# A planned instruction order for capped attention and a gated MLP: the planner's costs, landings and due times replaced

## The chip, the core and the metric

The kernel runs on one core of a Trainium2 chip. The core has five engines with a queue of instructions each: TensorE (PE, matrix products), VectorE (DVE, element-wise work), ScalarE (ACT, functions of one operand), GpSimd (POOL, hardly used here) and SyncE (SP, which issues nearly all transfers). An engine takes its instructions in the order in which they stand; one that waits holds up all behind it. The metric is the device time of one execution in microseconds (us), and lower is better.

## The reference, cut to what matters

```python
# 4 batches, 12 heads, 448 tokens, head size 64
scores = q @ k.T / sqrt(64)
scores = cap * tanh(scores / cap)
attn = exp(scores - max) ; attn = attn / (sum(attn) + 1e-9)
x = (attn @ v), heads side by side            # 1792 tokens x 768
g = x @ w_gate ; val = x @ w_val              # 768 x 1536 each
out = (g * sigmoid(g) * val) @ w_out          # 1536 x 768
```

The weights come as 64-bit floats and are narrowed to 32 bits on the chip. The large products run with operands that are split into two 16-bit halves, a high one and a low one.

## The kernel before

**Stages.** The attention comes first. A unit is one pair of heads of one batch; two units make a quad, and there are 12 quads. A quad has seven score tiles of 128 x 896: three of each unit and one (`MID`) with the rest of both. For each tile TensorE multiplies queries and keys (`qk`), ScalarE takes the tangent out of PSUM into a slot of SBUF (`tanh`) and the exponential in place (`exp`). Then TensorE multiplies with the values (`av` three times for each unit, `avt` for the rest) and with ones for the sums of the rows (`sum`), for which VectorE first adds three tiles (`sa`). The sums go over three transfers: `cp` copies them out of PSUM, `rl` spreads them over the partitions, `rec` takes the reciprocal on VectorE, `rs` writes it to memory, and `rld` reads it back for each unit, so that `x` can multiply the product that `xk` had copied out. The score tiles have two PSUM buffers (`sc`): the scores of a tile can be written when the tangent of the tile two before has read its own.

Behind the attention come 13 steps of gate and value products (`step`) and two passes of output products (`outs`). They use a scheme with seven products for a 2 x 2 block product; the blocks of x are differences of each other (`T1` to `T4`). For each product VectorE and ScalarE make a high half (`XH`, `wH`) and a low half (`XL`, `wL`) of the operands, and combine the partial results (`c1`, `c11`, `cu` and so on). The first step uses the first half of the batches only; in the second step the products of the second half begin. The weights are narrowed beside all this (`narrow`, `quarter`).

**The order.** `Plan.run` makes it when the kernel is built. Every operation has a cost on each engine that can run it, the operations that it depends on, the buffers that it takes, and a due time. The planner simulates the engines: of the operations that could start within 0.05 us of the earliest one, it takes the one with the earliest due time. The instructions are then written out in that order, and each engine keeps it, whatever the times turn out to be on the chip. TensorE's order in the attention stage isn't left to the planner: the list `line` at the end of the kernel ties each operation to the one before. Between the pieces of a quad there stand those of the quad before, in this order: one `qk`, three `av`, two `qk`, three `av`, one `qk`, `sum`, two `qk`, `avt`, one `qk`.

**Names that the change touches.** `QUAD` is the step of the quads in the due times, `tile_at` the due time of a tile in it (a seventh of `QUAD` each). `SWITCH` is a cost when TensorE goes from one kind of matmul to another, `LAG` and `LAT` are delays between the end of an operation and the start of one that depends on it, `FAR` is added to the landing of some transfers (`rl`, `rs`, `rld` are those of the reciprocals, `ld` are loads of weights), and `ISSUE` is the time in which SP issues one. `TAGS` gives each score tile the SBUF slot for its tangent. The due times of a tile at time z are z + 1.0 for `tanh` and z + 2.8 for `exp`.

Of the kernel before, what the change touches and what calls it, by code (L numbers as in the profile page):

```python
# [42 lines left out]
QUAD = 13.5  # L43
# [14 lines left out]
SWITCH = 0.17  # L58
# [21 lines left out]
class Plan:  # L80
# [3 lines left out]
    LAG = {  # L84
        ("PE", "PE"): 0.0, ("ACT", "ACT"): 0.13, ("DVE", "DVE"): 0.13, ("POOL", "POOL"): 0.13, ("ACT", "DVE"): 0.16,
        ("DVE", "POOL"): 0.16, ("ACT", "POOL"): 0.18, ("POOL", "ACT"): 0.07, ("POOL", "DVE"): 0.08, ("ACT", "PE"): 0.25,
    }

    FAR = {"rl": 1.4, "rs": 1.4, "rld": 1.4}
    ISSUE = {"rld": 0.96}  # L90
# [13 lines left out]
    def run(self):  # L104
# [69 lines left out]
        while ready:  # L174
            t0, cands = 1e18, []
            for k in ready:
# [5 lines left out]
                for t, d, e, x in o["opts"]:  # L182
                    s = max(t, r, free[e])
                    if e == "PE" and kind(k) != last:
                        s += SWITCH
# [36 lines left out]
def tile_capped_attention_gated_mlp(ctx: ExitStack, tc: tile.TileContext, qd, kd, vd, cap, eye, w1, w2, out):  # L222
# [104 lines left out]
    mm_us = 6 * 188 / 1000.0  # L327
# [95 lines left out]
    def blocks(w):  # L423
        g0, g1 = 2 * w * NCC, (2 * w + 1) * NCC
        for c in range(HALF):
# [14 lines left out]
            for p, (_, _, _, z) in PROD.items():  # L440
# [12 lines left out]
                if z in PLAIN:  # L453
                    n = 3 * PLAIN.index(z) + c
                    square(("qx", z, w, c), 2, win_at[3] + 10.0 * n + 5.0 * w, 0.58, lambda z=z, c=c: T["xs", z, w, c][:, 0], [("p", 3 + n // 2, 1, 4)], ("XH", z, w, c))

    def step(s):
# [46 lines left out]
        for half in range(2):  # L504
            if 1 in ws:
                square(key("q", half), 0, at[0] - 6.0 + 2.0 * half, 0.85, lambda half=half: gate(half).rearrange("p a b -> p (a b)"), full[half], ("XH", "B11", s // NFC, 0))
# [9 lines left out]
        for w in ws:  # L516
# [40 lines left out]
            for b in range(2):  # L557
# [22 lines left out]
                square(("qh", g, f), 3, max(end, z + 2.0) + 1.0, 0.58, lambda b=b, w=w: T["cc", s, w, b], [key("va", w, b)], ("XH", "B11", 0, 0) if s < NFC - 1 else ("oH", 0, 1, 0))  # L580
# [26 lines left out]
    def outs(pr):  # L607
# [54 lines left out]
        for n, (p, d) in enumerate(OUT_ORDER):  # L662
# [13 lines left out]
            if pr:  # L676
                square(("qo", p, d), 1, tp - 6.5, 0.85, lambda p=p, d=d: T["wf", "o", 1, p, d].rearrange("p a b -> p (a b)"), [("ld", "o", 1, p, d)], ("oH", 1, p, 0))
# [86 lines left out]
    TAGS, idle = {}, [f"w{n}" for n in range(6)] + ["B60", "B61", "B62", "B70", "B71"]  # L764
    for q in range(len(QUADS)):
        if q == len(QUADS) - 1:
            idle = [x for x in idle if x[0] == "B"] + ["B22", "B32", "B52"]
        old = TAGS.get(q - 1, [])
        TAGS[q] = [None] * NT
        for i in sorted(range(NT), key=lambda i: spot(q, i)):  # L770
            TAGS[q][i] = idle.pop(0)
# [477 lines left out]
```

## Time and profile before

| what | us |
|---|---|
| median of 3 runs | 603.34 |
| lowest and highest run | 602.14 and 603.51 |
| the profiled execution | 604.18 |
| span from its first to its last instruction | 602.3 |
| TensorE busy | 591.7 |
| VectorE busy | 505.9 |
| ScalarE busy | 418.4 |

The profiled execution's time has 1.9 us around its span. Times in the rows are counted from the start of the span. TensorE's matmuls are pipelined and their ends are modelled, so where consecutive matmuls start says more than how long they were busy. TensorE's granted clock is 0.999 of its full 2.4 GHz. PE is TensorE, DVE VectorE, ACT ScalarE, SPq SyncE's queue.

### The profile page before, as it was taken

What the parts mean: (1) busy time and instruction counts of PE and PEld (TensorE: products, weight loads), DVE (VectorE), ACT (ScalarE), POOL (GpSimd) and SP (SyncE); (2) the same over time, 40 slices, a digit from 0 to 9 for tenths busy, and PEclk for the clock granted to TensorE, in tenths of its full rate; (3) what the DMA queues carried; (4) which work ended last, traced back from release to release, by engine and by line L of the source; (5) the groups of instructions that cost most, each with busy time, mean ns of one, the idle gap of its engine ahead of it and who ended that gap; (6) DMA issues with size and microseconds to landing.
All of it is one profiled execution on the core that took longest, in us unless ns stands there. A gap on an engine that the chain in (4) does not pass through costs nothing.

```text
span 602.3 us, 9584 instructions
## 1 busy us (share of the span) xinstructions
PE 591.7 (98%) x3333; PEld 279.8 (46%) x3333; DVE 505.9 (84%) x869; ACT 418.4 (69%) x725; POOL 1.6 (0%) x11
## 2 busy tenths in 40 slices
PE   7999999999999999999999999999999999999997
PEld 2333333333345555555555555555455555555553
DVE  2678899899898998888989888989979999898840
ACT  6999989899858855756648476656757766685611
POOL 1000000000000000000000000000000000000000
PEclk9999999999999999999999999999999999999999
DMA  8676676755423365877786766586968598546121
GB/s 252 207 237 192 186 223 212 217 153 149 126 86 101 125 173 153 265 203 229 198 239 215 217 211 190 171 274 206 347 235 319 170 331 287 192 135 234 35 78 66
DMA packets 69598, 118.08 MB, mean 196 GB/s; under 512 B 13604, under 2 KB 47524, under 8 KB 69541
## 3 DMA queue, kind: packets, MB, share of 16 engines
q1 hardware_dynamic: 69362, 117.32, 61.4%
q8 instruction: 28, 0.46, 0.3%
q14 instruction: 30, 0.24, 0.1%
q10 hardware_dynamic: 146, 0.07, 0.0%
q0 software_dynamic: 32, 0.00, 0.0%
HBM read 81.79 MB, written 35.48 MB: 195 GB/s over the span
## 4 chain that ended last, share of the span: by engine, by line
PE 84%; DMA 6%; DVE 5%; ACT 2%; SPq 2%; issue 1%; ACTq 0%; DVEq 0%
PE b L528 10%; PE b L530 10%; PE b L529 10%; PE sc L886 7%; PE b L704 7%; PE b L703 7%; PE b L705 7%; PE av L831 6%; PE om L528 4%; PE om L530 4%; PE om L529 4%; DMA w<-w 3%; DMA r<-c 2%; PE b L918 2%; PE av L912 1%; PE om L704 1%
## 5 line engine op out<-in xcount | busy, mean ns | idle before, releaser
L528 PE MATMUL b<-A,w 128*128 128x448 f16 x252 | 88.8, 352 | 0.4 <-ACT c L255 0.4
L529 PE MATMUL b<-A,w 128*128 128x448 f16 x252 | 88.8, 352 | 0.0
L530 PE MATMUL b<-A,w 128*128 128x448 f16 x252 | 88.8, 352 | 0.0
L528 PEld LDWEIGHTS <-w 128*128 128x128 f16 x504 | 49.3, 98 | 46.8 <-issue 0.7
L529 PEld LDWEIGHTS <-w 128*128 128x128 f16 x504 | 49.3, 98 | 46.4 <-issue 0.7
L530 PEld LDWEIGHTS <-w 128*128 128x128 f16 x504 | 49.3, 98 | 46.0
L255 ACT ACTIVATE c<-b 128x448 f32<-128x448 f32 x54 | 29.0, 538 | 44.4 <-PE b L705 22.9
L528 PE MATMUL om<-B,w 128*128 128x448 f16 x144 | 50.8, 352 | 0.0
L529 PE MATMUL om<-B,w 128*128 128x448 f16 x144 | 50.8, 352 | 0.0
L530 PE MATMUL om<-B,w 128*128 128x448 f16 x144 | 50.8, 352 | 0.0
L886 PE MATMUL sc<-c,c 64*128 64x448 f32 (+1 forms) x192 | 45.2, 577 | 2.4 <-ACT w L890 1.5
L546 DVE TENSOR_TENSOR c<-c,b 128x448 f32<-128x448 f32 x60 | 37.1, 619 | 8.6 <-PE b L530 3.2
L262 DVE TENSOR_TENSOR A<-A,A 128x448 f16<-128x448 f32 (+3 forms) x55 | 43.7, 823 | 0.1
L255 ACT ACTIVATE w<-B 128x768 f16<-128x768 f32 x32 | 26.9, 840 | 22.9 <-PE b L705 17.9
L890 ACT ACTIVATE w<-sc 128x896 f32<-128x896 f32 x42 | 36.9, 917 | 7.2 <-PE sc L886 7.0
L890 ACT ACTIVATE B<-sc 128x896 f32<-128x896 f32 x42 | 36.9, 921 | 5.0 <-PE sc L886 4.9
L262 DVE TENSOR_TENSOR w<-B,w 128x768 f16<-128x768 f32 x39 | 37.0, 953 | 2.2 <-ACT w L255 2.2
L893 ACT ACTIVATE B<-B 128x896 f32<-128x896 f32 x42 | 38.4, 959 | 0.1
L893 ACT ACTIVATE w<-w 128x896 f32<-128x896 f32 x42 | 38.2, 955 | 0.1
L704 PE MATMUL b<-A,w 128*128 128x448 f16 x108 | 38.1, 352 | 0.0
L528 PE MATMUL b<-B,w 128*128 128x448 f16 x108 | 38.1, 352 | 0.0
L530 PE MATMUL b<-B,w 128*128 128x448 f16 x108 | 38.1, 352 | 0.0
(138 smaller groups left out, 1233.3 us busy)
## 6 DMA issues: line engine op xcount, KB each, us to landing
w<-w SPq DMA_DIRECT2D x72, 384.0 KB, 3.7
hidden<-c SPq DMA_DIRECT2D x48, 224.0 KB, 3.1
B<-w_S SPq DMA_DIRECT2D x24, 384.0 KB, 4.3
w<-wf SPq DMA_DIRECT2D x16, 384.0 KB, 4.9
B<-w SPq DMA_DIRECT2D x15, 384.0 KB, 3.4
th<-parts SPq DMA_DIRECT2D x48, 112.0 KB, 2.9
A<-hidden SPq DMA_DIRECT2D x12, 448.0 KB, 5.7
B<-hidden SPq DMA_DIRECT2D x12, 448.0 KB, 3.8
```

Source lines behind the costliest of these rows:

```text
L255: nc.scalar.activation(out_, in_, AF.Copy, scale=1.0 if scale is None else scale)
L262: ENG[e].tensor_tensor(out_, a, b, op=ALU.subtract)
L528: nc.tensor.matmul(o, lhsT=wh, rhs=xh, start=first, stop=False, skip_group_check=True)
L529: nc.tensor.matmul(o, lhsT=wl, rhs=xh, start=False, stop=False, skip_group_check=True)
L530: nc.tensor.matmul(o, lhsT=wh, rhs=xl, start=False, stop=end, skip_group_check=True)
L546: nc.vector.tensor_tensor(z, z, T["ps", s, w, b][:, :S], op=ALU.add)
L703: nc.tensor.matmul(o, lhsT=wh, rhs=xh, start=first, stop=False, skip_group_check=True)
L704: nc.tensor.matmul(o, lhsT=wl, rhs=xh, start=False, stop=False, skip_group_check=True)
L705: nc.tensor.matmul(o, lhsT=wh, rhs=xl, start=False, stop=end, skip_group_check=True)
L886: nc.tensor.matmul(z[rows, h, :S], lhsT=T["rk", w][r, keys], rhs=T["rq", w][r], start=True, stop=True)
L890: nc.scalar.activation(T["t", q, i], T["sc", q, i][:, :, :S], AF.Tanh, scale=icapr)
L893: nc.scalar.activation(T["t", q, i], T["t", q, i], AF.Exp, scale=capr)
```

## The change

The diff replaces constants of the planner and two rules in it.

- The step of the quads goes from 13.5 to 13.1; the due time of an exponential from z + 2.8 to z + 5.0.
- The switch cost of TensorE depends on the kind of matmul that it leaves.
- Delays between dependent operations on ScalarE and VectorE are 0.04, and after an operation the engine is free 0.1 (ScalarE) or 0.085 (VectorE) before its end. Before, it was free at the end, and a dependent one came 0.13 to 0.16 later.
- The transfers of the reciprocals land 2.0 later than their data would by the planner's rate, not 1.4; loads of weights 1.5 later, not 0. Issuing takes other times, 2.45 for the four transfers of a quad's values, not 0.48.
- The slots for the tangents come from a ring of eleven in order of the tiles, with seven fixed ones for the last quad. Before, slots were handed on from a list of idle ones.
- Some costs: squares 0.08 more, `tanh` 0.917 and `exp` 0.953, `sum` 1.27, and 189 ns for a matmul of the products.

The operations, their dependences, their tiles and TensorE's order in the attention stage stay.

```diff
-QUAD = 13.5
+QUAD = 13.1
...
-SWITCH = 0.17
+SWITCH = {"sc": 0.206, "av": 0.15, "sh": 0.16, "sum": 0.0, "mm": 0.16}
...
-    LAG = {
-        ("PE", "PE"): 0.0, ("ACT", "ACT"): 0.13, ("DVE", "DVE"): 0.13, ("POOL", "POOL"): 0.13, ("ACT", "DVE"): 0.16,
-        ("DVE", "POOL"): 0.16, ("ACT", "POOL"): 0.18, ("POOL", "ACT"): 0.07, ("POOL", "DVE"): 0.08, ("ACT", "PE"): 0.25,
-    }
-
-    FAR = {"rl": 1.4, "rs": 1.4, "rld": 1.4}
-    ISSUE = {"rld": 0.96}
+    LAG = {("PE", "PE"): 0.0, ("ACT", "PE"): 0.08, ("DVE", "PE"): 0.08}
+    LAG |= {(a, b): 0.04 for a in ("ACT", "DVE") for b in ("ACT", "DVE")}
+    OVERLAP = {"ACT": 0.1, "DVE": 0.085}
+
+    FAR = {"rl": 2.0, "rs": 2.0, "rld": 2.0, "ld": 1.5}
+    ISSUE = {"rld": 1.26, "loadv": 2.45, "rl": 0.65, "rs": 0.4, "ld": 0.45, "st": 0.54}
...
-                        s += SWITCH
+                        s += SWITCH[last]
...
-                free[e] = s + self.ISSUE.get(k[0], 0.48)
+                free[e] = s + self.ISSUE.get(k[0], 0.48) * (2 if k[0] == "loadq" and d > 1.0 else 1)
...
-                free[e] = s + d
+                free[e] = s + d - self.OVERLAP.get(e, 0.0)
...
-    mm_us = 6 * 188 / 1000.0
+    mm_us = 6 * 189 / 1000.0
...
-    TAGS, idle = {}, [f"w{n}" for n in range(6)] + ["B60", "B61", "B62", "B70", "B71"]
...
+    RING = [*(f"w{n}" for n in range(6)), "B60", "B61", "B62", "B70", "B71"]
...
-            tag = TAGS[q][i]
+            tag = (["B22", "B32", "B52", "B60", "B61", "B62", "B70"][spot(q, i)] if q == len(QUADS) - 1 else RING[(NT * q + spot(q, i)) % len(RING)])
...
-            op(("tanh", q, i), z + 1.0, {"ACT": 0.92}, tanh, [("qk", q, i)], [(tag, users)])
-            op(("exp", q, i), z + 2.8, {"ACT": 0.95}, expo, [("tanh", q, i)])
+            op(("tanh", q, i), z + 1.0, {"ACT": 0.917}, tanh, [("qk", q, i)], [(tag, users)])
+            op(("exp", q, i), z + 5.0, {"ACT": 0.953}, expo, [("tanh", q, i)])
...
-        op(("sum", q), av_at(q, 2), {"PE": 1.15}, sums, [("sa", u, 1), ("sa", v, 1), ("exp", q, MID)], [("b2", [("cp", q)])])
+        op(("sum", q), av_at(q, 2), {"PE": 1.27}, sums, [("sa", u, 1), ("sa", v, 1), ("exp", q, MID)], [("b2", [("cp", q)])])
```

## Rows read from the trace of the kernel before

**Rows 1.** The page, busy times: engine, us, share of the span, instructions.

```profile
PE 591.7 (98%) x3333; PEld 279.8 (46%) x3333; DVE 505.9 (84%) x869; ACT 418.4 (69%) x725; POOL 1.6 (0%) x11
```

**Rows 2.** The chain that ended last: start, duration, what (us).

```profile
27.34 1.70 PE sc L886 x12
...
40.40 1.70 PE sc L886 x12
...
62.63 1.27 PE b L918 x24
...
67.41 6.07 DMA r<-c
...
89.35 1.27 PE b L918 x24
...
102.41 1.27 PE b L918 x24
...
107.24 4.91 DMA r<-c
...
128.90 1.27 PE b L918 x24
...
137.39 5.18 DMA parts<-r
```

**Rows 3.** Windows: stretch, length, busy us (instructions) of each engine, clock, DMA.

```profile
core 0: us, PE busy (x) PEld busy (x) DVE busy (x) ACT busy (x) POOL busy (x), PEclk, DMA share, GB/s
...
154.00:168.00 14.00, 12.65 (x110) 4.60 (x108) 14.00 (x24) 13.31 (x19) 0.00 (x0) 1.00 0.34 103
...
196.00:203.00 7.00, 7.00 (x39) 3.62 (x38) 7.00 (x15) 5.37 (x12) 0.00 (x0) 1.00 0.10 35
...
392.00:424.00 32.00, 31.59 (x168) 16.24 (x166) 27.93 (x55) 17.08 (x40) 0.00 (x0) 1.00 0.80 244
```

**Rows 4.** TensorE's timeline: start, us, line, operation, tiles, [idle before <-releaser].

```profile
4.22 3.91 PE L886 MATMUL sc<-c,c 64*128 64x448 f32 x12
...
10.66 1.92 PE L886 MATMUL sc<-A 64*128 64x448 f32 x8 [1.46 <-ACT w L890]
...
14.96 1.02 PE L886 MATMUL sc<-c,c 64*128 64x448 f32 x4
...
159.69 0.59 PE L886 MATMUL sc<-c,c 64*64 64x448 f32 x2 [0.78 <-ACT B L890]
...
161.24 4.73 PE L831 MATMUL av<-B,B 128*64 128x448 f32 x24 [0.57 <-DVE B L257]
```

**Rows 5.** ScalarE's timeline (L890 tangent, L893 exponential, L255 cast), in five places.

```profile
8.02 1.78 ACT L893 ACTIVATE w<-w 128x896 f32<-128x896 f32 x2
9.70 0.91 ACT L890 ACTIVATE w<-sc 128x896 f32<-128x896 f32 x1
...
13.07 1.73 ACT L890 ACTIVATE w<-sc 128x896 f32<-128x896 f32 x2
...
153.45 0.52 ACT L255 ACTIVATE w<-wf 128x384 f16<-128x384 f32 x1 [1.57 <-DMA wf<-w]
153.88 0.93 ACT L893 ACTIVATE B<-B 128x896 f32<-128x896 f32 x1
```

**Rows 6.** VectorE's timeline (L932 reciprocal, L257 cast, L262 subtraction).

```profile
73.50 0.24 DVE L932 RECIPROCAL r<-r 128x14 f32<-128x14 f32 x1 [2.65 <-DMA r<-c]
...
152.34 0.56 DVE L257 CAST w<-wf 128x768 f16<-128x768 f32 x1 [1.96 <-DMA wf<-w]
...
194.44 5.97 DVE L262 TENSOR_TENSOR B<-B,B 128x448 f16<-128x448 f32 x11
```

**Rows 7.** SyncE's queue, the first load of gate weights (L466).

```profile
148.60 0.55 SPq L466 DMA_DIRECT2D wf<-w  x1
```

**Rows 8.** TensorE's timeline, the last matmul of the second half's first product.

```profile
195.15 0.35 PE L530 MATMUL om<-B,w 128*128 128x448 f16 x1
```

**Rows 9.** The page's DMA issues: operands, queue, count, KB each, us to landing.

```profile
parts<-r SPq DMA_DIRECT2D x12, 7.0 KB, 1.5
```

More of the change, by code (lines that the diff above doesn't have):

```diff
@@ L454, in blocks @@
                     n = 3 * PLAIN.index(z) + c
-                    square(("qx", z, w, c), 2, win_at[3] + 10.0 * n + 5.0 * w, 0.58, lambda z=z, c=c: T["xs", z, w, c][:, 0], [("p", 3 + n // 2, 1, 4)], ("XH", z, w, c))
+                    square(("qx", z, w, c), 2, win_at[3] + 10.0 * n + 5.0 * w, 0.66, lambda z=z, c=c: T["xs", z, w, c][:, 0], [("p", 3 + n // 2, 1, 4)], ("XH", z, w, c))
     def step(s):
@@ L505, in step @@
             if 1 in ws:
-                square(key("q", half), 0, at[0] - 6.0 + 2.0 * half, 0.85, lambda half=half: gate(half).rearrange("p a b -> p (a b)"), full[half], ("XH", "B11", s // NFC, 0))
+                square(key("q", half), 0, at[0] - 6.0 + 2.0 * half, 0.93, lambda half=half: gate(half).rearrange("p a b -> p (a b)"), full[half], ("XH", "B11", s // NFC, 0))
         last = [2, 5, 3, 4]
@@ L579, in step @@
                 op(key("va", w, b), max(end + 0.2, z + 2.2), {"DVE": 0.62}, va, deps)
-                square(("qh", g, f), 3, max(end, z + 2.0) + 1.0, 0.58, lambda b=b, w=w: T["cc", s, w, b], [key("va", w, b)], ("XH", "B11", 0, 0) if s < NFC - 1 else ("oH", 0, 1, 0))
+                square(("qh", g, f), 3, max(end, z + 2.0) + 1.0, 0.66, lambda b=b, w=w: T["cc", s, w, b], [key("va", w, b)], ("XH", "B11", 0, 0) if s < NFC - 1 else ("oH", 0, 1, 0))
                 op(("hst", g, f), max(end, z + 2.0) + 1.2, {"SP": 0.64}, hst, [key("va", w, b)])
@@ L676, in outs @@
             if pr:
-                square(("qo", p, d), 1, tp - 6.5, 0.85, lambda p=p, d=d: T["wf", "o", 1, p, d].rearrange("p a b -> p (a b)"), [("ld", "o", 1, p, d)], ("oH", 1, p, 0))
+                square(("qo", p, d), 1, tp - 6.5, 0.93, lambda p=p, d=d: T["wf", "o", 1, p, d].rearrange("p a b -> p (a b)"), [("ld", "o", 1, p, d)], ("oH", 1, p, 0))
             def wH(e, p=p, d=d, n=n):
@@ L762, in av_at @@
         return quad_at[q] + (QUAD * (1.3 + 0.3 * n) if q < len(QUADS) - 1 else QUAD + 2.0 + 2.3 * n)
-    TAGS, idle = {}, [f"w{n}" for n in range(6)] + ["B60", "B61", "B62", "B70", "B71"]
[L765 to L771, printed above, removed]
-            if old and i in (2, 4, MID):
-                idle += [x for x in {2: old[1:4], 4: old[4:], MID: old[:1]}[i] if x[0] == "B" or q < len(QUADS) - 1]
+    RING = [*(f"w{n}" for n in range(6)), "B60", "B61", "B62", "B70", "B71"]
     def pair(u, q):
@@ L1104, in tile_capped_attention_gated_mlp @@
         avs = lambda z: [("av", z, j) for j in range(3)]
-        line += now[:1] + avs(u) + now[1:3] + avs(v) + now[3:4] + [("sum", q - 1)] + now[4:6] + [("avt", q - 1)] + now[6:]
+        line += now[0:1] + avs(u) + now[1:3] + avs(v) + now[3:4] + [("sum", q - 1)] + now[4:6] + [("avt", q - 1)] + now[6:7]
     for a, b in zip(line, line[1:]):
```

## The prediction

> **What bounds the kernel now.** I read the page's busy times first: TensorE is busy 98% of the span [rows 1]. That alone does not say where time can be had, so next came the chain of work that ended last, which is a list of TensorE's pieces with few others between them [rows 2]. It falls into two stages. In the attention stage the matmuls of one quad repeat with a fixed step: the score pieces at 27.34 and 40.40 us are 13.06 us apart. In the product stage TensorE has no gap at all: it is busy 7.00 of 7.00 us and 31.59 of 32.00 us in the two stretches shown [rows 3]. The diff changes no matmul, and the order of TensorE's attention work is written out by hand and stays. So the end can move only by the time in which TensorE waits for somebody. I looked for these waits one by one.
>
> In attention, two steps run from the row at 62.63 to that at 89.35 us, 26.72 us where 2 x 13.06 = 26.12 were due: 0.60 lost. From 102.41 to 128.90 it is 26.49, so 0.37 lost [rows 2]. TensorE's timeline shows the last two: 0.78 us for a tangent on ScalarE at 159.69 and 0.57 us for a copy on VectorE at 161.24 [rows 4]; together 1.35. In the product stage there is the 0.41 us of 32.00 - 31.59 [rows 3]. And at the start the first quad's tiles crawl: the scores for the second quad begin at 14.96 us only, with a wait of 1.46 us at 10.66 on the way [rows 4]. Not counting the start, that is 0.60 + 0.37 + 1.35 + 0.41 = 2.73 us.
>
> **The change part by part.** *Exponentials behind the next tangents.* A tangent's due time is its tile's time plus 1.0, an exponential's moves from plus 2.8 to plus 5.0, and tiles are 13.1/7 = 1.87 apart. So the exponential of tile j comes after the tangent of j+2 (3.74 + 1.0 = 4.74, under 5.0) and ahead of that of j+3 (6.61). This matters where ScalarE is behind, which is the first quad. Two score buffers hold TensorE to ScalarE's tangents: tile j+2 is multiplied when the tangent of j has ended. Before, ScalarE ran both exponentials from 8.02 (1.78 us), then the third tangent at 9.70, and tangents five and six from 13.07, ending at 13.07 + 1.73 = 14.80 [rows 5]; just behind that end stands the first tile of quad two, at 14.96 [rows 4]. With the new due times I lay it out by hand from the same rows. One exponential from 8.02; a pair of them takes 1.78 and a pair of tangents 1.73, and instructions on ScalarE overlap by about 0.1, so one costs 0.84 and one tangent 0.82. Then: third tangent 8.86, fourth 9.68, exponential 10.50, the small one for the epsilon 0.1, fifth tangent 11.44, exponential 12.26, sixth 13.10 to 14.02. Its end moves from 14.80 to 14.02. Allowing for whether each tile's scores are there in time, I take 0.8 to 0.9 and put down 0.9 as an estimate; bounds 0 (a tangent misses its scores each time) and 1.46 (the one wait at 10.66 goes whole).
>
> In the steady steps the new due time costs nothing: seven tangents and exponentials at 0.82 + 0.84 are 11.6 us on ScalarE, under TensorE's 13.06, and tangents are taken first. The cover is thin at one place: from the end of the fifth tile's scores TensorE has another tile and one tail product, about 1.7 us by the 1.70 for eight score matmuls [rows 2], before it needs that tile's tangent, which takes 0.92. A tangent that finds ScalarE in an exponential of 0.84 would be late by up to 0.1. If that came in each of eleven steps it costs 1.1 us; none to 1.1 are the bounds, and I take 0.
>
> *Overlaps and pace.* The planner now lets an independent instruction of ScalarE start 0.1 us and one of VectorE 0.085 us before the end of the one ahead. The rows bear that out: eleven VectorE subtractions of 0.62 us take 5.97 us, not 6.82, which is 0.085 for each of ten joints [rows 6], and two tangents of 0.92 take 1.73 [rows 5]. It changes no work, only the order; what it corrects is large, since some 85 VectorE instructions stand between 152 and 203 us, that is 85 x 0.085 = 7 us which the old plan believed missing. The Trainium skill, VectorE: DVE Perf Modes, section "The DRAIN you can't avoid", says that the next operation does not start until the pipe is empty. By that rule VectorE would have those 7 us less, and the new order would be too tight there; the 5.97 us disagree with it, so it has a chance below 1 in 100 here.
>
> *Issue and landing.* SP's issue of a quad's values counts 2.45 us instead of 0.48, loads of narrowed weights land 1.5 us later, and the three transfers of a quad's reciprocals 0.6 us later each. This moves the VectorE and ScalarE instructions that wait for them back in their queues, and behind them nothing is stuck. The trace has the two waits that this is about. At 73.50 VectorE has stood 2.65 us before a reciprocal [rows 6], whose transfer was issued at 67.41 and took 6.07 [rows 2]; it never catches up before the accumulator copies that TensorE waits for next. And the first gate weights are issued at 148.60 [rows 7] and reach VectorE at 152.34, after 1.96 us of idling [rows 6], and ScalarE at 153.45 after 1.57 us, with tangents and exponentials queued behind that cast [rows 5]. The two waits at 159.69 and 161.24 follow from it. I take two thirds of each: 0.6 of 0.97 and 0.9 of 1.35. All or none are the bounds; the transfer of a reciprocal took 6.07 and 4.91 us [rows 2], while the plan now has about 4 us, so a part must stay.
>
> *Slots for tangents* go round a ring of eleven. A slot's last readers are those of eleven tiles before; the nearest case, tile five of a quad on tile one of the quad before, was read by products that stand right behind the quad's first tile, over 5 us ahead. Nothing: if that cover is gone, one tangent of 0.92 is late. *Switch costs, pace 13.1, 189 ns* change due times only: 0.
>
> *Product stage.* Of the 0.41 us I take 0.2. A re-laid order of some 600 VectorE instructions may have a new wait or two in it; I put 0.4 for that, bounds 0 and what the third rival below costs.
>
> Sum: -0.9 - 0.6 - 0.9 - 0.2 + 0.4 = -2.2 us. The profiled execution took 604.18 us with a span of 602.3, 0.84 above the median of 603.34; against the median I forecast 603.34 - 2.2 = 601.1 us. A difference of 0.3%, 1.8 us, is about what a measurement of this kernel can tell from none.
>
> **The rivals.** *Waits move* (for it: VectorE is busy 14.00 of 14.00 us from 154 to 168 [rows 3], so what is taken from one wait may come out behind the next). The start's 0.9 stays, of the rest little: 603.34 - 0.9 = 602.4, between 601.6 and 605.0.
>
> *Nothing changes*: the tangents' scores are never there early, and the pairs of two tangents and two exponentials stay as they are. Against it, the scores of the third tile are through at 4.22 + 3.91 = 8.13 us [rows 4], and the first of the two exponentials from 8.02 [rows 5] ends after that. 603.3.
>
> *VectorE is late into the second half of the batches*, the side that is slower. The first product of that half has its last matmul at 195.15 us [rows 8], and the subtraction that it reads ends at 194.44 + 0.62 = 195.06 [rows 6]: 0.1 us in hand. From there VectorE is busy 7.00 of 7.00 us to 203 [rows 3]. The operands come by the last quad's reciprocal, over three transfers in a row. The plan now has each 0.6 later, and gate weights 1.5: if VectorE's queue puts 3 x 0.6 + 1.5 = 3.3 us of less urgent work ahead of these subtractions, TensorE waits 3.2 us, and with the start's 0.9 that gives 603.34 + 2.3 = 605.6. It decides from 0.1 us on. One of these transfers was in truth both slow and fast: 5.18 us at 137.39 [rows 2], 1.5 us by the list of issues [rows 9], so no single figure fits. Against it: the 7 us that the old plan believed missing on VectorE are there in the new one. The Trainium skill, DMA: Bandwidth & Descriptors, section "Latency and other measured facts", says the fixed part of a transfer shrinks with a lighter load; the two figures agree, and by it the longer landing would be wrong exactly in the quiet stretch at 168 us and later.
>
> **How the numbers follow.** Forecast 0.52, waits move 0.30, nothing changes 0.03, VectorE late 0.15. The forecast's own range goes from all waits gone, 0.9 + 0.97 + 1.35 + 0.41 = 3.63, so 599.7, to 601.5. The range of all reaches up to 605.0, the upper end of moved waits, and leaves out the late VectorE: 599.5 to 605.0. Faster by over 0.3% is the forecast, 0.52; within it 0.33; slower 0.15.
>
> **What the profile after would show.** Right: the first tile of quad two near 14.0 us; no VectorE idling of 2 us for a reciprocal or for the first gate weights; the two waits at 160 us gone; the first product of the second stage near 165.7 instead of 168.1, and the same TensorE pace behind it. Wrong: a wait of TensorE on VectorE's subtractions some 25 us into the product stage, steps longer than 13.06 us with waits on tangents, or new idle time at narrowed weights.

## The result and the profile after

The changed kernel takes 607.9 us (median, 606.95 to 609.12) where the kernel before took 602.96 beside it on the same chip (602.14 to 603.51). The ratio is 1.0084, interval 1.0062 to 1.0107: 0.8% slower. 601.1 us was forecast, with a range to 605.0. The profiled execution after took 607.89 us with a span of 606.1; before's took 604.18 with 602.3, so the two profiles differ by 3.8 us of span.

The page of after, span and busy times:

```profile
span 606.1 us, 9542 instructions
PE 593.3 (98%) x3333; PEld 279.7 (46%) x3333; DVE 516.3 (85%) x903; ACT 399.3 (66%) x691; POOL 1.6 (0%) x11
```

Against [rows 1] TensorE has the same 3333 matmuls. VectorE has 34 instructions more and ScalarE 34 fewer: the planner gave VectorE more of the work that either can do, 29 of them operations of narrowing (`nA`, `nB`).

Before any cause comes the place. I cut both spans at the first score matmul, the first product and the last product's end:

| stretch | before | after | difference |
|---|---|---|---|
| start to first score matmul | 4.22 | 4.22 | 0 |
| attention, to the first product | 163.87 | 161.19 | -2.68 |
| products, to the end of the last matmul | 429.77 | 436.57 | +6.80 |
| tail | 4.43 | 4.11 | -0.32 |
| span | 602.3 | 606.1 | +3.8 |

So the attention gained about what was forecast (-2.4), and the products lost 6.8 us where +0.2 was forecast (-0.2 and +0.4). TensorE's timeline of after shows the attention's gains (columns as in [rows 4]):

```profile
9.73 1.83 PE L876 MATMUL sc<-A 64*128 64x448 f32 x8 [0.62 <-ACT w L880]
13.92 1.02 PE L876 MATMUL sc<-c,c 64*128 64x448 f32 x4 [0.76 <-ACT w L880]
...
158.56 4.73 PE L821 MATMUL av<-B,B 128*64 128x448 f32 x24
...
165.41 0.36 PE L527 MATMUL b<-A,w 128*128 128x448 f16 x1
```

Quad two starts at 13.92, not 14.96, the two waits at 160 us in [rows 4] are gone, and the first product comes at 165.41 instead of 168.09. ScalarE's timeline of after has the order that the prediction laid out (L880 tangent, L883 exponential):

```profile
7.93 0.94 ACT L883 ACTIVATE w<-w 128x896 f32<-128x896 f32 x1
8.77 1.71 ACT L880 ACTIVATE w<-sc 128x896 f32<-128x896 f32 x2
10.36 0.96 ACT L883 ACTIVATE w<-w 128x896 f32<-128x896 f32 x1
11.20 0.93 ACT L880 ACTIVATE w<-sc 128x896 f32<-128x896 f32 x1
...
12.93 0.93 ACT L880 ACTIVATE w<-sc 128x896 f32<-128x896 f32 x1
```

One exponential, two tangents, one exponential, then tangents five and six with an exponential between; the sixth ends at 13.86, where 14.02 was worked out and 14.80 was before [rows 5].

Now the loss. Windows of the product stage, first before, then after (columns as in [rows 3]):

```profile
168.00:203.00 35.00, 35.00 (x189) 18.10 (x186) 32.13 (x60) 24.55 (x49) 0.00 (x0) 1.00 0.26 82
203.00:447.00 244.00, 243.59 (x1289) 125.90 (x1288) 218.40 (x417) 154.83 (x354) 0.00 (x0) 1.00 0.70 218
```

```profile
168.00:203.00 35.00, 34.52 (x182) 17.52 (x180) 34.30 (x65) 23.68 (x48) 0.00 (x0) 1.00 0.30 88
203.00:447.00 244.00, 239.06 (x1259) 122.95 (x1257) 219.40 (x434) 138.11 (x319) 0.00 (x0) 1.00 0.70 212
447.00:600.00 153.00, 153.00 (x811) 79.13 (x809) 124.87 (x157) 84.42 (x135) 0.00 (x0) 1.00 0.58 197
```

TensorE stands 4.94 of the 244 us from 203 to 447, where it stood 0.41, and 0.48 of the 35 us ahead of it, where it stood 0; from 447 on it has no gap. The clock is full in all of them. Consecutive product matmuls start 0.189 us apart, and what is above that I call excess from here on: 0.58 us in all before and 7.38 after. That is the 6.8. Of the 7.38, 1.15 lie at 167 to 201 us, and 6.23 in eight places from 282 to 445 us (1.65 at 282, 0.64 at 298, 0.68 at 347, 0.58 at 371, 1.26 at 396, 0.72 at 426, 0.38 at 436 and 0.34 at 445). So who is late there? The waits between 203 and 446 us (engine, operand and line, releaser: us in total, times, longest), before:

```profile
DVE wf L1031 <- DMA w<-wf: 1.1, 4, 0.5
```

and after (L1021 is the same line of code):

```profile
DVE wf L1021 <- DMA w<-wf: 10.1, 12, 2.3
...
PE om L527 <- DVE c L545: 2.7, 5, 1.1
...
DVE c L256 <- DMA hidden<-c: 1.6, 2, 1.3
...
PE b L527 <- DVE c L256: 1.5, 1, 1.5
```

The first line is the new one. L1021 adds or subtracts two narrowed blocks of output weights (`S`, on VectorE; called a sum from here on); it writes its sum over one of the blocks, and that block has just been sent to memory by a transfer, `w<-wf`. The sum can't start until that *store* is through. VectorE reaches it too early and stands there for 10.1 us in all, with everything that is queued behind it. VectorE's timeline of one such place, and TensorE's behind it:

```profile
387.74 0.56 DVE L971 SCALAR_TENSOR_TENSOR wf<-wf,w 128x384 int32<-128x384 int32 x1
389.68 0.56 DVE L1021 TENSOR_TENSOR wf<-wf 128x384 f32<-128x384 f32 x1 [1.38 <-DMA w<-wf]
390.16 0.35 DVE L256 CAST w<-wf 128x384 f16<-128x384 f32 x1
...
394.89 0.61 DVE L565 TENSOR_TENSOR c<-th,c 128x448 f32<-128x448 f32 x1
395.42 0.61 DVE L545 TENSOR_TENSOR c<-c,om 128x448 f32<-128x448 f32 x1
```

```profile
394.64 0.35 PE L529 MATMUL b<-A,w 128*128 128x448 f16 x1
396.09 0.35 PE L527 MATMUL om<-B,w 128*128 128x448 f16 x1 [1.10 <-DVE c L545]
```

VectorE is idle for 1.38 us up to 389.68. From there it works, with no wait that the profile puts down to anybody, through eleven more instructions to the addition at 395.42 (L545, of a product onto what was copied out before), which ends at 396.03, and TensorE, which has waited 1.10 us for it, goes on at 396.09. The chain of waits for that stretch goes the same way back and ends in the store:

```profile
385.81 3.78 DMA w<-wf
...
389.68 0.56 DVE wf L1021
```

The chains behind the other seven places, read in the same way, go back to such a store at 298, 347 and 426 us (3.81, 3.72 and 4.13 us long; at 426 by way of ScalarE, and the kernel before has a wait of 0.57 at the same matmuls), to the store of a hidden tile at 282 (5.50 us), to a load of weights at 371, to a load of hidden tiles at 436, and at 445 into VectorE's own queue. So weight stores stand behind 3.3 of the 6.23 us and a store of a hidden tile behind 1.65.

The store in the rows took 3.78 us. The planner has it through at the earliest 1.125 + 0.55 + 0.73 = 2.4 us after its issue: the diff raises what it adds to a landing (`FAR`) for loads and reciprocals and adds nothing for stores. The page's DMA issues of the kernel before (operands, queue, count, KB each, us from issue to landing in the middle of those whose landing the profile has, which are 10 of 24, 10 of 48 and 3 of 12) had the number already:

```profile
w<-wf SPq DMA_DIRECT2D x24, 192.0 KB, 3.8
...
hidden<-c SPq DMA_DIRECT2D x48, 224.0 KB, 3.1
...
A<-hidden SPq DMA_DIRECT2D x12, 448.0 KB, 5.7
```

The second is the store of a finished tile of the hidden layer (`hst`, 2.5 us in the plan) and the third the load of such tiles for the output products (`hld`, 3.1 in the plan). The Trainium skill, DMA: Bandwidth & Descriptors, section "Latency and other measured facts", gives about 2 us as the fixed cost of a transfer; with the planner's 0.55 for the data that is an estimate of 2.6 us, near the plan, and the 3.78 us in the trace are 1.2 us over it.

### The profile page after: what moved, and what is told of

The parts are those of the page before. It is cut to its first block, busy times and chain, and to the rows that moved or that the text cites. A ratio compares the mean times of both kernels' runs of the same rounds, so it can differ in the third digit from the quotient of the medians.

```text
span 606.1 us, 9542 instructions
## 1 busy us (share of the span) xinstructions
PE 593.3 (98%) x3333; PEld 279.7 (46%) x3333; DVE 516.3 (85%) x903; ACT 399.3 (66%) x691; POOL 1.6 (0%) x11
## 4 chain that ended last, share of the span: by engine, by line
PE 49%; DVE 28%; DMA 12%; issue 5%; ACT 3%; SPq 1%; DVEq 0%; ACTq 0%
PE sc L876 9%; PE av L821 7%; PE b L704 7%; PE b L702 7%; PE b L703 7%; DMA w<-wf 6%; DVE w L967 3%; DVE c L545 3%; DVE w L261 3%; DVE wf L971 3%; DVE c L565 3%; DVE ss L261 2%; DMA hidden<-c 2%; DMA w<-w 2%; PE b L908 2%
## 5 line engine op out<-in xcount | busy, mean ns | idle before, releaser
L527 PE MATMUL b<-A,w 128*128 128x448 f16 x252 | 88.8, 352 | 2.4 <-DVE c L256 1.8
L528 PE MATMUL b<-A,w 128*128 128x448 f16 x252 | 88.8, 352 | 0.0
L529 PE MATMUL b<-A,w 128*128 128x448 f16 x252 | 88.8, 352 | 0.0
L254 ACT ACTIVATE c<-b 128x448 f32<-128x448 f32 x49 | 26.1, 535 | 48.2 <-PE b L704 29.0
L880 ACT ACTIVATE B<-sc 128x896 f32<-128x896 f32 x42 | 37.6, 922 | 5.2 <-PE sc L876 4.8
L321 ACT ACTIVATE A<-c 128x448 f16<-128x448 f32 x48 | 27.5, 572 | 20.3 <-DVE c L565 20.0
L880 ACT ACTIVATE w<-sc 128x896 f32<-128x896 f32 x42 | 37.4, 916 | 4.8 <-PE sc L876 4.6
L545 DVE TENSOR_TENSOR c<-c,b 128x448 f32<-128x448 f32 x60 | 36.9, 615 | 2.8 <-ACT A L321 1.4
L883 ACT ACTIVATE w<-w 128x896 f32<-128x896 f32 x42 | 38.8, 954 | 0.1
L883 ACT ACTIVATE B<-B 128x896 f32<-128x896 f32 x42 | 38.6, 957 | 0.2
L560 ACT ACTIVATE th<-c 128x448 f32<-128x448 f32 x48 | 26.1, 565 | 18.6 <-DVE c L545 18.6
L704 PE MATMUL b<-A,w 128*128 128x448 f16 x108 | 38.1, 352 | 0.0
L528 PE MATMUL b<-B,w 128*128 128x448 f16 x108 | 38.1, 352 | 0.0
L703 PE MATMUL b<-A,w 128*128 128x448 f16 x108 | 38.1, 352 | 0.0
```

The source lines that it names most:

```text
L527: nc.tensor.matmul(o, lhsT=wh, rhs=xh, start=first, stop=False, skip_group_check=True)
L528: nc.tensor.matmul(o, lhsT=wl, rhs=xh, start=False, stop=False, skip_group_check=True)
L529: nc.tensor.matmul(o, lhsT=wh, rhs=xl, start=False, stop=end, skip_group_check=True)
L545: nc.vector.tensor_tensor(z, z, T["ps", s, w, b][:, :S], op=ALU.add)
L703: nc.tensor.matmul(o, lhsT=wl, rhs=xh, start=False, stop=False, skip_group_check=True)
L704: nc.tensor.matmul(o, lhsT=wh, rhs=xl, start=False, stop=end, skip_group_check=True)
```

## The experiments

**Theory:** the plan takes a store to be through too early. Before, the planner's slow clock for VectorE (no overlap of instructions, 0.13 to 0.16 between dependent ones) pushed the additions late enough; the change mends the clock and not the stores. **Rivals:** VectorE has too much to do (34 instructions more); the new plan is too tight all through the product stage, whatever the transfer; the exponentials' due time; the landings of the last quad's reciprocals (the prediction's own slower case).

All runs in one table; exp_back and ld_old were executed twice each, the other changed ones four to twelve times. The ratio is against runs of the kernel before on the same chip, "idle before sums" is VectorE's idle time just ahead of line L1021 over the whole span, first product and excess are read from the profile as above.

| kernel | median us | ratio (interval) | first product | excess | idle before sums |
|---|---|---|---|---|---|
| before | 602.96 | | 168.09 | 0.58 | 1.1 |
| after | 607.90 | 1.0084 (1.0062 to 1.0107) | 165.41 | 7.38 | 10.1 |
| old_behind | 603.64 | 1.0015 (0.9997 to 1.0033) | 164.74 | 3.14 | 3.2 |
| st_later | 602.87 | 1.0000 (0.9981 to 1.0018) | 164.59 | 2.68 | 0.1 |
| st_only | 603.67 | 1.0014 (0.9996 to 1.0033) | 164.95 | 3.95 | 0.0 |
| hld_later | 601.26 | 0.9978 (0.9960 to 0.9995) | 164.44 | 2.25 | 0.1 |
| narrow_act | 608.73 | 1.0085 (1.0061 to 1.0109) | 165.84 | 7.13 | 16.8 |
| exp_only | 611.15 | 1.0159 (1.0112 to 1.0206) | 168.92 | 5.35 | 2.2 |
| exp_back | 610.76 | 1.0134 (1.0096 to 1.0173) | 164.34 | 9.68 | 13.5 |
| ovl_only | 613.87 | 1.0185 (1.0144 to 1.0226) | 173.57 | 3.64 | 4.8 |
| land_only | 615.58 | 1.0210 (1.0183 to 1.0236) | 164.87 | 13.39 | 0.8 |
| ld_old | 614.06 | 1.0186 (1.0148 to 1.0223) | 173.43 | 6.04 | 0.6 |
| r_old | 604.05 | 1.0020 (1.0002 to 1.0038) | 167.68 | 1.98 | 0.3 |
| last_r | 603.65 | 1.0013 (0.9998 to 1.0027) | 164.45 | 3.07 | 0.3 |

**Later stores.** The changed kernel, with stores of weights and of hidden tiles through 1.5 us later in the plan (st_later), and with those of weights alone (st_only):

```diff
-    FAR = {"rl": 2.0, "rs": 2.0, "rld": 2.0, "ld": 1.5}
+    FAR = {"rl": 2.0, "rs": 2.0, "rld": 2.0, "ld": 1.5, "st": 1.5, "hst": 1.5}   # st_later
+    FAR = {"rl": 2.0, "rs": 2.0, "rld": 2.0, "ld": 1.5, "st": 1.5}               # st_only
```

> The changed kernel with stores of weights and of hidden blocks landing 1.5 us later in the planner, as the change has it for loads alone. Theory 1a, VectorE stands in line for stores that the planner thinks landed (10.1 us of idling before the sums of output weights, 1.1 before the change): those waits fall under 4 us and the time to 601 to 604 us. Theory 1b, the waits for stores are only where a lack of slack comes out: they move to other operations and the time stays at 606 to 609 us.

> The changed kernel with stores of weights alone landing 1.5 us later in the planner; hidden blocks as in the changed kernel. If the stores of weights are the cause, the waits before the sums of output weights go as in the run that moved both, and the time is 602 to 604 us. If the landing of hidden blocks has its share (the wait of 1.48 us at 282 us was for one), 604 to 606 us, with waits on copies that overwrite a hidden block.

By the two ratios st_later is 0.8% faster than the changed kernel, some 5 us: as much as the change lost. No wait of VectorE for a store is left in the list, and TensorE's busy time from 203 to 447 us is back at 242.76:

```profile
203.00:447.00 244.00, 242.76 (x1283) 125.43 (x1282) 222.33 (x439) 142.44 (x328) 0.00 (x0) 1.00 0.73 220
```

That is 4.7 of the 6.8 us of excess; 2.1 are left. The total is that of the kernel before because the attention gains more (3.50 us, not 2.68) and the tail behind the last matmul is 1.3 us longer than before, for which no run gives a reason.

st_only takes most of the same off (0.7%, some 4 us), and the idle time before the sums is gone as well. What it leaves is at 432 and 441 us, 1.89 and 0.90 us of excess. The chain of st_only up to there goes back to one load of hidden tiles, which took 7.26 us where the plan has 3.1 at the earliest:

```profile
419.74 7.26 DMA A<-hidden
...
428.50 1.00 DVE A L261
```

**VectorE's load.** The changed kernel, with the two narrowing operations drawn back to ScalarE by a handicap of 0.3 us on VectorE:

```diff
-    BIAS = {}
+    BIAS = {("nA", "DVE"): 0.3, ("nB", "DVE"): 0.3}
```

> The changed kernel with 0.3 us put on VectorE's side in the choice of an engine for the first two steps of narrowing: 76 of 144 of them go to VectorE and not 104. Theory 1c, the 29 instructions that went over from ScalarE fill VectorE: 602 to 604 us. If it is not the load of VectorE but its order, 606 us or more.

VectorE has 881 instructions instead of 903, and the time is that of the changed kernel: 608.73. The idle time before the sums is even more, 16.8 us; that would fit a VectorE that reaches them sooner with less to do, which isn't shown by itself. The load falls as a cause.

**The old rules behind the attention.** The changed kernel, whose planner goes back to the old delays, no overlap and the old landings of all but the reciprocals for what it places behind 164 us:

```diff
...
+    CUT = 164.0
...
-                    t = max(t, end[x] + self.LAG.get((eng[x], e), self.LAT))
+                    t = max(t, end[x] + (self.LAG if end[x] < self.CUT else self.OLD_LAG).get((eng[x], e), self.LAT))
...
-                end[k] = dma_free + 0.73 + self.FAR.get(k[0], 0.0)
+                end[k] = dma_free + 0.73 + (self.FAR.get(k[0], 0.0) if s < self.CUT or k[0][0] == "r" else 0.0)
...
-                free[e] = s + d - self.OVERLAP.get(e, 0.0)
+                free[e] = s + d - (self.OVERLAP.get(e, 0.0) if s < self.CUT else 0.0)
```

> The changed kernel, but what the planner starts after 164 us of its own time goes by the old costs: old delays between dependent operations, no overlap of instructions, no added landing for weight loads. Theory 1, the product stage's new order is bad because the new costs leave VectorE no slack behind the attention: the attention keeps its gain of 2.7 us, the product stage loses under 1 us, 600.0 to 601.5 us. Theory 2, VectorE is late because the attention ends 2.7 us earlier, whatever the costs behind it: the product stage loses 4 us or more all the same, 604 to 608 us.

603.64: most of the loss goes as well, though the products keep 2.6 us of it and the time lies above the 600.0 to 601.5 that was expected. The excess of 3.14 us has no part at the sums, before which VectorE still stands 3.2 us; most of it lies at 181, 193 and 475 to 477 us. So a clock that is too slow does cover the stores, as the theory says. By itself this run would also fit the rival that the new plan is too tight as such; st_later decides against that for 4.7 of the 6.8 us, since it keeps the tight plan, and leaves it open for the 2.1 us that remain.

**The exponentials alone, and all but them.** The kernel before with the new due time, and the changed kernel with the old one:

```diff
-            op(("exp", q, i), z + 2.8, {"ACT": 0.95}, expo, [("tanh", q, i)])
+            op(("exp", q, i), z + 5.0, {"ACT": 0.95}, expo, [("tanh", q, i)])     # exp_only, in the kernel before
-            op(("exp", q, i), z + 5.0, {"ACT": 0.953}, expo, [("tanh", q, i)])
+            op(("exp", q, i), z + 2.8, {"ACT": 0.953}, expo, [("tanh", q, i)])    # exp_back, in the changed kernel
```

> The kernel before with the exponential's due time alone moved to plus 5.0. As predicted for the first quad: the first tile of quad two starts 0.9 us earlier, near 14.0 us, and 602.1 us if nothing else moves. If the re-laid order behind it brings waits of its own, the start is still 0.9 earlier and the total anywhere from 602 to 606 us.

> The changed kernel with the exponential's due time back at plus 2.8. By the prediction, from the first score tile to the first tile of quad two it takes 10.6 us again and not 9.7. If the start doesn't depend on it, 9.7 us stays. The product stage is laid out anew and may wait more or less than the 7.4 us of the changed kernel.

At the place that the prediction costed the two agree with it. From the first tangent to the first tile of quad two it takes 8.82 us in the kernel before and 8.55 in the three others with the old due time; with the new one it takes 7.78 in the changed kernel and 7.60 to 7.83 in the nine others. That is 0.8 to 1.0 us. (The first tangent starts anywhere from 4.9 to 6.1 us, so this is counted from there; the expectation of exp_back counted from the first scores. By that count it measured 9.62 us, not the 10.6 that was expected, as its first tangent starts 0.93 us earlier than the changed kernel's; why that start moves isn't known.) But neither time followed it. exp_only is 1.6% slower, outside the 602 to 606 us that were expected: with the planner's old costs the same due time sets waits of 1.88, 0.89 and 1.93 us at 55, 69 and 111 us, and 5.35 us of excess behind. exp_back lost 9.68 us in the products, with 13.5 us before the sums, more than the changed kernel. A due time of ScalarE in the attention has changed how long VectorE stands for stores 200 us later; I can't price it apart from that.

**The pace alone, and the landings alone.** The kernel before with the new delays and overlaps (ovl_only), and with all landings and issue times including those of stores and hidden loads (land_only); both keep the old due time of the exponentials and the old slots:

```diff
...
+    LAG = {("PE", "PE"): 0.0, ("ACT", "PE"): 0.08, ("DVE", "PE"): 0.08}           # ovl_only
+    LAG |= {(a, b): 0.04 for a in ("ACT", "DVE") for b in ("ACT", "DVE")}
+    OVERLAP = {"ACT": 0.1, "DVE": 0.085}
...
-                free[e] = s + d
+                free[e] = s + d - self.OVERLAP.get(e, 0.0)                              # ovl_only
...
+    FAR = {"rl": 2.0, "rs": 2.0, "rld": 2.0, "ld": 1.5, "st": 1.5, "hst": 1.5, "hld": 2.0}   # land_only
+    ISSUE = {"rld": 1.26, "loadv": 2.45, "rl": 0.65, "rs": 0.4, "ld": 0.45, "st": 0.54}                             # land_only
```

> The kernel before with two parts of the change alone: the shorter delays between dependent operations and the overlap of instructions on ScalarE and VectorE. Theory 1, it is VectorE's faster clock in the planner that takes away the slack by which stores had landed: idling of VectorE before the sums of output weights over 6 us (1.1 before, 10.1 in the changed kernel) and over 3 us of waits of TensorE in the product stage, 605 to 609 us. Rival, the waits come from the later landing of loads and the longer issues, which this kernel hasn't: idling under 3 us and 600 to 603 us.

> The kernel before with landings and issues alone: those of the change, and also stores, hidden blocks and their loads later, as in the run that beat the kernel before. Delays, no overlap and the exponentials' due time stay as before. Theory, the planner of before had two errors that offset each other, VectorE too slow and landings too early: with the landings alone put right, VectorE waits for no transfer (under 2 us before the sums and narrowings, 201 to 447 us), but the order is laid out for an engine slower than it is, and the gain of the attention stage comes in part: 600 to 605 us. Rival, the landings were the only error that cost time: 601.3 us plus 0.9 for the first quad, 602.2 us or less, with the attention's end 1.5 us or more earlier than before.

Each alone is some 11 to 13 us slower than the kernel before, which is outside all that was expected of either. With the right pace and the old landings VectorE runs into loads that aren't there. Before the sums it stands 4.8 us, less than the 6 that were expected for stores; its largest wait between 14 and 168 us is for loads of weights (4.0 us in the kernel before):

```profile
DVE B L258 <- DMA w<-w: 17.5, 10, 3.9
```

and the first product comes at 173.57. With the right landings and the old pace the attention is good (first product at 164.87), VectorE waits 2.7 us for transfers in the product stage (9.6 in the kernel before, from 203 to 446 us), and 13.39 us of excess come from operands that are simply late in its queue. TensorE's timeline of land_only at the worst of these places, and three windows around it:

```profile
481.18 0.35 PE L704 MATMUL b<-B,w 128*128 128x448 f16 x1
484.61 0.47 PE L705 MATMUL b<-B,w 128*128 128x448 f16 x1 [3.07 <-DVE B L262]
484.87 0.58 PE L703 MATMUL b<-B,w 128*128 128x448 f16 x1
```

```profile
478.00:481.00 3.00, 3.00 (x18) 1.54 (x17) 2.48 (x4) 2.96 (x5) 0.00 (x0) 1.00 0.87 235
481.00:484.60 3.60, 0.53 (x3) 0.19 (x2) 3.60 (x5) 3.46 (x4) 0.00 (x0) 1.00 0.62 218
484.60:488.20 3.60, 3.59 (x11) 1.47 (x11) 3.60 (x4) 0.00 (x0) 0.00 (x0) 0.53 0.46 156
```

**Two landings taken back.** The changed kernel without the later loads (ld_old); and st_later with the reciprocals' transfers at the old 1.4 (r_old):

```diff
-    FAR = {"rl": 2.0, "rs": 2.0, "rld": 2.0, "ld": 1.5}
+    FAR = {"rl": 2.0, "rs": 2.0, "rld": 2.0}                                       # ld_old
+    FAR = {"rl": 1.4, "rs": 1.4, "rld": 1.4, "ld": 1.5, "st": 1.5, "hst": 1.5}     # r_old
```

> The changed kernel without the 1.5 us on loads of weights. If that shift is what brings stores and sums of output weights close together, VectorE's idling before the sums falls from 10.1 to under 5 us. If it is VectorE's faster clock in the planner, it stays over 7 us. In the attention stage the first gate weights are expected too early again, so the waits of TensorE near 157 to 161 us come back, 0.8 us or more.

> The run with later stores, and the three transfers of the reciprocals landing 1.4 later as before the change, not 2.0. By the prediction's third rival the three later landings push VectorE's subtractions back, and the waits of TensorE from 180 to 205 us fall from 1.1 us to under 0.3: 601.5 to 602.5 us. Otherwise they stay at 0.8 us or more and the time at 602.5 to 603.5 us.

Without the loads' 1.5 us the first product comes at 173.43, 8.0 us later than in the changed kernel. VectorE then waits for the loads, in the attention and in the product stage (two views of ld_old, 14 to 168 and 203 to 446 us), and is so late that the sums find their stores through (0.6 us):

```profile
DVE B L258 <- DMA w<-w: 15.2, 7, 3.3
```

```profile
DVE wf L258 <- DMA w<-w: 9.2, 13, 1.8
```

In the changed kernel these two are 6.4 and 0.9 us. By what was written beforehand the fall to 0.6 us before the sums would mean that the loads' shift brings stores and sums together; but a VectorE that is 8 us late would show the same, so this run doesn't tell the two apart. This one entry is worth about 8 us in the attention once the pace is right. The reciprocals' 0.6 is worth 3.1 there: r_old has its first product at 167.68, not 164.59, with waits of TensorE at 54, 157 and 160 us. It gets part of that back: it has no excess at the transition, where st_later has 1.1 us between 166 and 200, and the median is 604.05. So the waits fell as the prediction's third rival would have it, and the time didn't, since the attention ends 3.1 us later; that lateness could by itself be what clears the transition.

**The last quad, and the hidden loads.** st_later with the loads of hidden tiles 2.0 us later (hld_later), and that with the last quad's reciprocals at 1.0 (last_r):

```diff
-    FAR = {"rl": 2.0, "rs": 2.0, "rld": 2.0, "ld": 1.5}
+    FAR = {"rl": 2.0, "rs": 2.0, "rld": 2.0, "ld": 1.5, "st": 1.5, "hst": 1.5, "hld": 2.0}   # hld_later, last_r
+    LAST = {("rl", 11), ("rs", 11), ("rld", 20), ("rld", 23)}                                # last_r
-                end[k] = dma_free + 0.73 + self.FAR.get(k[0], 0.0)
+                end[k] = dma_free + 0.73 + (1.0 if k in self.LAST else self.FAR.get(k[0], 0.0))         # last_r
```

> The run with later stores, and the loads of hidden blocks for the output products landing 2.0 us later in the planner too. If their landing (7.26 us for one, in the run with weight stores alone) is what makes TensorE wait at 430 to 442 us, the 1.6 us of waits there fall under 0.5 and the time is 601 to 602 us. Otherwise the waits stay and it is 602.5 to 603.5 us.

> The run before, and the last quad's three transfers of the reciprocals landing 1.0 us later in the planner, not 2.0 (the other quads' stay at 2.0). Only the third rival's place is touched: the waits of TensorE from 180 to 205 us go from 1.1 to under 0.4 us, the attention's end stays within 0.3 us, and the time is 0.5 to 1.0 us under that of the run with hidden loads later. If the waits there have other reasons, they stay.

hld_later takes 601.26 us, 0.22% under the kernel before (interval 0.05 to 0.40%) and the fastest of all kernels here; the time is the one that was expected. Its page, and its window of the product stage:

```profile
span 600.3 us, 9543 instructions
PE 591.9 (99%) x3333; PEld 279.8 (47%) x3333; DVE 515.0 (86%) x900; ACT 398.7 (66%) x694; POOL 1.6 (0%) x11
```

```profile
203.00:447.00 244.00, 243.38 (x1286) 125.62 (x1284) 222.33 (x436) 143.09 (x330) 0.00 (x0) 1.00 0.72 219
```

But the waits at 430 to 445 us are down only from 1.56 us in st_later to 1.11, not under 0.5, and of the 1.9 us by which its span is shorter than st_later's 1.3 are the tail behind the last matmul. Against st_later the gain of the hidden loads alone is inside both intervals, so what they are worth isn't shown. last_r doesn't remove the waits behind the first step: 0.50 us at 192 and 1.02 at 200 are there, and 0.88 came up at 477 to 480 us. It takes 603.65, some 2 us more than hld_later where 0.5 to 1.0 less was expected. So the landings of the last quad aren't what makes the second half's operands late.

**All together.** Five kernels have the new pace and later weight stores throughout (st_later, st_only, hld_later, r_old, last_r): VectorE stands at most 0.3 us before the sums, and they take 601.3 to 604.1 us. Five have the new pace and the old stores throughout (the changed kernel, narrow_act, exp_back, ovl_only, ld_old): 607.9 to 614.1 us, the first three with 10 to 17 us before the sums, the last two with less and late for their loads. With the step in st_later, where two entries of the planner move and nothing else, this shows the early stores as the cause of most of the loss.

## Why the prediction was right and wrong

**The start: right.** Forecast -0.9, measured 13.92 - 14.96 = -1.04, by the very order that was laid out.

**The rest of the attention: the sum came out by luck.** Forecast -1.5 (-0.6 for the steps, -0.9 for the two waits at 160 us), measured -2.68 + 1.04 = -1.64, of which the steps have nothing and the two waits all.

The steps: from the sums of quad four (counted from zero) to those of quad eight it took 53.21 us before and 53.17 after, where 4 x 13.06 = 52.24 was due. The prediction put this loss down to VectorE's waits for the reciprocals' transfers. Those waits are gone, and VectorE stands for the transfer that reads the reciprocals back instead (at 61, 63 and 113 us; 0.4 us in all before). VectorE's waits from 14 to 168 us, before, then after:

```profile
DVE r L932 <- DMA r<-c: 4.0, 3, 2.6
```

```profile
DVE A L839 <- DMA th<-parts: 4.2, 3, 2.1
```

The loss has moved: the two steps from the sums of quad three lose 0.28 us (0.60 before) and those from quad six nothing (0.37), but the one step between them loses 0.64, where it lost nothing.

The two waits: from the sums of quad eight to the first product it went from 39.26 to 37.66 us, -1.60, and both waits went whole. The sign that the prediction named for it didn't come: VectorE still stands for the first gate weights, 1.78 us where it was 1.96 [rows 6].

```profile
152.42 0.56 DVE L256 CAST w<-wf 128x768 f16<-128x768 f32 x1 [1.78 <-DMA wf<-w]
```

So VectorE's idle time isn't what set the wait for a tangent. ScalarE's is, and that half of the prediction's mechanism holds. Before, ScalarE stood 1.57 us at 153.45 for a cast of gate weights with tangents behind it [rows 5]. After, no cast stands between the tangents, and ScalarE waits there for TensorE instead. r_old has the cast at that place again (ScalarE, first after, then r_old):

```profile
153.99 0.92 ACT L880 ACTIVATE B<-sc 128x896 f32<-128x896 f32 x1 [0.71 <-PE sc L876]
```

```profile
155.83 0.52 ACT L254 ACTIVATE w<-wf 128x384 f16<-128x384 f32 x1 [2.73 <-DMA wf<-w]
156.25 0.90 ACT L880 ACTIVATE B<-sc 128x896 f32<-128x896 f32 x1
```

In the three kernels where ScalarE stands for that cast at 153 to 156 us (before 1.57, land_only 1.34, r_old 2.73), TensorE waits for tangents at 157 to 160 us (0.78; 0.64; 1.22 and 0.58); in the other eleven there is neither. Which entry of the planner moves the cast isn't settled: r_old has the reciprocals' old landing and the cast in the way, but exp_only and ovl_only, with the same old landing, don't, and there the stretch takes 37.77 and 37.97 us. The new due time of the exponentials isn't needed for it (37.66 in exp_back). From quad two to the sums of quad four it is 60.66 us in both kernels: the steady steps cost nothing more there, as forecast.

**The pace: right.** After's VectorE starts the next instruction ahead of the end of the one before (in its timeline above the addition at 389.68 is 0.56 us long and is followed at 390.16, 0.08 early). The Trainium skill's rule in VectorE: DVE Perf Modes, section "The DRAIN you can't avoid", which the prediction gave less than 1 in 100, doesn't hold for these rows as the prediction took it; its first paragraph adds that an operation which isn't held starts earlier, and the early start in these rows agrees with that.

**The step that failed: "A re-laid order of some 600 VectorE instructions may have a new wait or two in it; I put 0.4 for that".** The product stage measured +6.8 where the prediction's two terms make +0.2, and the sign of the whole went with it: -2.68 + 6.80 - 0.32 = +3.8 in the profiles. (Of the 0.41 us in the old product stage nothing came back either: the wait at 422 us is there after, at 426, with 0.72 of excess.) The prediction asked of each landing that the diff raises whether the raise is right. It didn't ask which landings the diff leaves. The change takes some 7 us of believed slack out of VectorE between 152 and 203 us alone, by the prediction's own 85 x 0.085, and goes on to do so at the same rate; a transfer whose landing is still planned too early can then be met early. With the stores planned 1.5 us later 4.7 of the 6.8 us went (st_later). That the stores were such a case stood in the page of the kernel before, 3.8 us against 2.4, and the wait at L1031 was in its list with 1.1 us. The bound for the unknown cost was taken from a rival with another mechanism (3.2 us at one place) and not from the 24 stores of 192 KB with 1.4 us each (33.6 us if each were met in full; VectorE stood before 12 of the 24 sums, for 10.1 us).

**The rivals.** The slower one ("VectorE is late into the second half of the batches") had the right side and a wrong cause. Its place does show waits, at 186 to 201 us, but they are 1.15 us together with that at 167, not 3.2, and last_r leaves them there. What pushes them isn't settled. Of the kernels made from the changed one with later stores, they are gone only in r_old, where the attention ends 3 us later. The prediction set two landings of one kind side by side, 5.18 us and 1.5 [rows 9]; the second is that of a single transfer, issued at 163.83 us, the only one of the twelve whose landing the profile has. "Waits move" came true in a way that the prediction hadn't priced: not the attention's waits, but new ones 100 us and more behind it. Among the signs of being wrong the prediction did list "new idle time at narrowed weights", which is where it was.

**What stays open.** What the exponentials' due time is worth in the whole (exp_only and exp_back are both slower than what they start from, for waits far behind); why the steps at 75 to 128 us keep 0.9 us of waits after, while they take 52.25 us in exp_back and 52.3 and 52.8 in st_later and st_only, which differ from it in the stores' landing alone; what makes the operands late at 186 to 201 us; and the other 2.1 us of the products' excess that st_later keeps.

## What to carry to other kernels

An order that is planned ahead can rest on errors that hold each other up: a clock that is too slow for an engine covered transfers that were planned too fast. Mending the pace and a part of the landings made this kernel 0.8% slower, the pace alone 1.9% and the landings alone 2.1%, while the pace with all the landings made it 0.2% faster. So ahead of such a change set each kind of transfer in the page's list of DMA issues beside its landing in the plan, stores too where something overwrites what is being stored, and look above all at those that the change leaves as they are. And price a re-laid order by the waits that it could meet (count of transfers times the error of each), not by the waits that it is meant to remove. Such a count is an upper bound and no forecast: here it gives 33.6 us for the stores, and the products lost 6.8.

## What the runs showed of the hardware

TensorE's clock can fall behind a wait. In land_only TensorE stood 3.07 us up to 484.61; the granted clock was 1.00 in the windows ahead and 0.53 in the 3.6 us behind, near the 1.2 GHz level, and eleven matmuls took those 3.59 us. So that wait cost more than itself. The length of the wait alone doesn't decide it: in ld_old the clock fell behind a wait of 2.09 us at 111.87 and stayed at 1.00 behind one of 2.83 us at 70.43. TensorE's timeline of ld_old at both places, and a window behind each:

```profile
70.43 2.48 PE L821 MATMUL av<-B,B 128*64 128x448 f32 x12 [2.83 <-DVE A L256]
...
111.87 0.97 PE L821 MATMUL av<-w,B 128*64 128x448 f32 x4 [2.09 <-DVE B L256]
```

```profile
70.40:74.00 3.60, 3.57 (x18) 1.46 (x20) 3.60 (x6) 0.67 (x2) 0.00 (x0) 1.00 0.79 229
112.80:116.40 3.60, 3.60 (x12) 1.01 (x10) 3.60 (x8) 0.36 (x1) 0.00 (x0) 0.53 0.76 226
```

The waits of the changed kernel behind the first quad, of up to 1.48 us, left the clock at 1.00.

Landings of one kind of transfer differ widely. The load of hidden tiles of 448 KB lands after 5.7 us in the middle (before, three landings) and took 7.26 us in st_only; one of the reciprocals' transfers of 7 KB took 1.5 us in the kernel before, issued at 163.83 us, and 5.18 at 137.39 [rows 2]. The page's 4.0 after is the middle of two landings:

```profile
parts<-r SPq DMA_DIRECT2D x12, 7.0 KB, 4.0
```

One figure for each kind was enough for the waits on stores to go: with 1.5 added, the plan has them through after 3.9 us, where they took 3.8 in the middle. It was not enough for the loads of hidden tiles: with 2.0 added the plan has 5.1 us, and in hld_later one that took 7.93 stands behind a wait with 0.2 us of excess at 430 us. The two places behind it (0.3 at 438 and 0.6 at 444 us) go back through VectorE's and ScalarE's queues.
